# A fused attention and two-MLP kernel: weight preparation, operand splits, input loads and output transposes are given other places in the program

## The chip, the cores and the metric

The kernel runs on one core of a Trainium2 chip. The metric is the device time of one execution in microseconds (us). The program has five instruction streams, one for each engine: PE (TensorE, matmuls and their weight loads), DVE (VectorE), ACT (ScalarE), POOL (GpSimd, here used almost only to issue DMAs) and SP (SyncE, which issues DMAs). Each engine works through its stream in order and waits on semaphores where it needs another's result.

## The reference, cut to what matters

```python
def _attn_ref(q, k, v, mem_k, mem_v):          # 4 x 8 heads, 768 positions, 64 wide, in chunks of 32
    ...                                        # softmax over 16 left, 32 own, 8 right and 8 memory positions

def _moe_ref(x, w_gate, w_val, w_out, rms_g):  # 3072 tokens x 512, d_ff 1536
    xn = x / np.sqrt(np.mean(x * x, axis=-1, keepdims=True) + 1e-06) * rms_g
    g = xn @ w_gate
    return (g * (1.0 / (1.0 + np.exp(-g))) * (xn @ w_val) @ w_out)

def _moe2_ref(x, w_in, w_out):                 # d_ff 2048
    h = x @ w_in
    g = np.where(h >= 1, h, np.where(h <= -1, 0.0, (h + 1) ** 2 / 4.0))
    return g @ w_out
```

The output of the attention goes through the first MLP and then through the second. The weights arrive as 64-bit floats and are turned into 32-bit floats on the chip. For accuracy every 32-bit operand x is split into a high part and a rest, x = hi + lo, and a product takes three matmuls: hi·hi, hi·lo and lo·hi.

## The kernel before, in words

The 3072 tokens are six tiles of 512 (`NTT` = 6). The program runs through these stages:

1. An opening stage with the attention of the first tokens (a hand-written list, `ORDER`).
2. Tiles 0 to 3, one by one, through the first MLP (lines 847 to 876). A tile has 12 column blocks f; a block is 12 matmuls of 128x512 for the gate, 12 for the values and 12 for the output of the block before. Each block has three slots (`slot`, line 767), in which attention steps for later tiles and background steps are laid between the matmuls. Tiles 1 to 3 make 108 slots.
3. Tiles 4 and 5 as a pair through the first MLP. A pair uses a scheme with seven instead of eight products of half-size blocks (Strassen in Winograd's form), for which sums of operands must be formed. The projection has 12 blocks of seven products of six matmuls (`seven`, `proj1`); the output has 7 x 6 blocks of six matmuls (`Out.run`).
4. Three pairs of tiles through the second MLP, each with 8 projection blocks of seven products (`proj2`) and 7 x 8 output blocks.

**Background steps.** The weights of stages 3 and 4 have to be converted, split and summed, and stored in DRAM in the order of the seven products. This work is a list of 376 steps (`steps`, filled by `w1_steps`, `w1o_steps` and `w2_steps`). `conv_step(n)` adds n to a counter and runs as many steps as are due. A slot of tiles 1 to 3 adds `PACE`, a product of stage 3 adds `PACE2`; what remains runs in one go at line 1122. A period of 28 steps prepares one column block and one row block of the second MLP: four loads of 512 KB by POOL (line 276), conversions on ACT and DVE (lines 289, 142 to 148), splits (292, 295), sums (197 to 207), and stores by POOL (303, 209). Loads reuse three buffers `w64`, conversions three buffers `tu`, so a load waits for the stores out of its buffer, and a conversion for the stores out of `tu`. All this stands in the same in-order streams as the work of the products.

**A projection block** (`seven`, line 900). PE makes products 0 and 3; ACT copies the first from PSUM bank A into bank B (line 908), and product 4 is accumulated on top of it, so PE's third product waits for this copy. ACT also copies the second product (line 909), DVE adds (912, 915), and `proj2` then forms the piecewise function with DVE clamps (945), ACT squares (946) and DVE maxima (950). At its end a block issues the load of the weights for the block after the next (`load_wp`, line 799, 1.8 MB, two buffers).

**An output stage** (`Out.run`). Before a block's six matmuls, its operand h is split by ACT (993) and DVE (995) into a ring of buffers, a few blocks ahead; the first ones are split by `ahead` (999) before the last projection block. `load_wo` (815) loads weights four pairs of blocks ahead. Between blocks stand the steps of `x_steps`, which form the sums and splits of the next pair's input y; they are spread by the queue `xq`. The input of the next pair is loaded by `load_y` (793, twice 1 MB on SP) after the projection. Each pair's output is four quarters (j, o), which `turn` (1076) transposes on PE and writes to DRAM: two during the output stage, two after the first two projection blocks of the next pair.

## Time and profile before

| | us |
|---|---|
| median of 3 runs | 1230.75 (1229.84 to 1232.29) |
| the profiled execution | 1235.12 |
| span of its instructions | 1233.3 |
| PE busy | 1149.3 (93%) |
| DVE busy | 865.9 (70%) |
| ACT busy | 619.9 (50%) |
| POOL busy | 155.1 (13%) |

Busy time of PE is not PE at its peak: matmuls overlap, and one that follows a gap or runs at the lower clock counts as longer. More is read from the time that equal numbers of matmuls take in different stages, and from what PE waited for between two of them. Idle time of another engine matters only where PE waits for it in the end.

### The profile page before, as it was taken

How to read it: one execution, taken by the hardware profiler on the slowest of the kernel's cores; microseconds unless marked ns; L12 is line 12 of the kernel's file. 1: busy time of each engine (PE TensorE's matmuls, PEld its weight loads, DVE VectorE, ACT ScalarE, POOL GpSimd, SP SyncE). 2: the span in 40 equal slices, each digit the busy share in tenths (PEclk: the TensorE clock that was granted, in tenths of full speed). 3: DMA queues.
4: the chain of work that ended last, by engine and by line, in shares of the span. 5: the costliest groups of instructions: out<-in, count | busy, mean ns of one | idle time of the engine just before them, and what ended most of it. 6: DMA issues, size and time to landing. Idle time of an engine off the chain costs nothing.

```text
span 1233.3 us, 20567 instructions
## 1 busy us (share of the span) xinstructions
PE 1149.3 (93%) x7909; PEld 919.7 (75%) x7909; DVE 865.9 (70%) x1494; ACT 619.9 (50%) x1096; POOL 155.1 (13%) x239
## 2 busy tenths in 40 slices
PE   6889999999999999787797999989999899999998
PEld 4677877777777788566575768868878778777786
DVE  5889766576657668666568767787757878567855
ACT  4676756565567655333333634446433455334453
POOL 2200012222222332222322000000000000000000
PEclk8899999999999999899998999999999999999999
DMA  8566377788776866998878675566754576653465
GB/s 294 186 204 207 122 266 258 243 283 280 257 269 226 264 222 209 310 357 297 306 262 327 215 247 188 200 247 192 207 185 180 186 249 184 196 186 151 123 196 160
DMA packets 93969, 281.77 MB, mean 228 GB/s; under 512 B 11440, under 2 KB 34480, under 8 KB 87472
## 3 DMA queue, kind: packets, MB, share of 16 engines
q1 hardware_dynamic: 66992, 207.05, 50.4%
q0 software_dynamic: 19200, 65.03, 14.8%
q10 hardware_dynamic: 7680, 8.39, 2.0%
q8 instruction: 62, 1.02, 0.3%
q14 instruction: 35, 0.29, 0.1%
HBM read 201.26 MB, written 79.17 MB: 227 GB/s over the span
## 4 chain that ended last, share of the span: by engine, by line
PE 65%; DVE 11%; DMA 11%; issue 6%; ACT 4%; POOL 2%; ACTq 0%; SPq 0%; DVEq 0%; POOLq 0%
PE ps_y L1045 11%; PE ps_g L1045 8%; PE ps_g L584 6%; PE ps_g L586 5%; PE ps_g L585 5%; DMA w2p_d<-w 3%; PE ps_y L584 3%; PE ps_y L586 2%; PE ps_y L585 2%; PE ps_b L888 2%; PE ps_g L888 2%; PE ps_b L890 2%; PE ps_b L889 2%; DMA w<-in_w_dram 2%; PE ps_g L890 2%
## 5 line engine op out<-in xcount | busy, mean ns | idle before, releaser
L1045 PE MATMUL ps_y<-r,wo 128*128 128x512 f32 x720 | 173.7, 399 | 10.9 <-DMA wo<-w2o_d 5.4
L1045 PEld LDWEIGHTS ps_y<-r,wo 128*128 128x128 f32 x720 | 137.8, 192 | 43.6 <-ACT ps_g L1006 6.1
L995 DVE TENSOR_TENSOR r<-h,r 128x512 fp32r<-128x512 f32 x180 | 121.4, 687 | 54.6 <-ACT r L993 54.3
L584 PE MATMUL ps_g<-xh,wall 128*128 128x512 f32 x384 | 156.1, 407 | 0.1
L586 PE MATMUL ps_g<-xh,wall 128*128 128x512 f32 x384 | 150.7, 392 | 0.1
L585 PE MATMUL ps_g<-xl,wall 128*128 128x512 f32 x384 | 150.5, 392 | 0.0
L993 ACT ACTIVATE r<-h 128x512 fp32r<-128x512 f32 x180 | 108.3, 625 | 68.4 <-PE ps_y L1045 17.4
L946 ACT ACTIVATE t<-t,half 128x512 f32<-128x512 f32 x96 | 66.9, 720 | 132.7 <-DVE t L945 132.7
L1045 PE MATMUL ps_g<-r,wo 128*128 128x512 f32 x540 | 128.1, 392 | 2.7 <-DVE r L995 1.5
L1045 PEld LDWEIGHTS ps_g<-r,wo 128*128 128x128 f32 x540 | 100.5, 188 | 27.1 <-DVE r L995 4.9
L888 PE MATMUL ps_g<-wall 128*128 128x512 f32 x198 | 80.7, 408 | 23.5 <-ACT ps_g L908 13.5
L888 PE MATMUL ps_b<-wall 128*128 128x512 f32 x202 | 80.6, 399 | 12.6 <-ACT ps_b L908 5.0
L586 PEld LDWEIGHTS ps_g<-xh,wall 128*128 128x128 f32 x384 | 72.6, 189 | 16.3 <-DVE wall L117 0.5
L584 PEld LDWEIGHTS ps_g<-xh,wall 128*128 128x128 f32 x384 | 72.7, 189 | 15.8 <-ACT wall L116 0.3
L585 PEld LDWEIGHTS ps_g<-xl,wall 128*128 128x128 f32 x384 | 72.9, 190 | 13.6
L584 PE MATMUL ps_y<-hh,wall 128*128 128x512 f32 x192 | 78.0, 406 | 3.5 <-ACT hh L116 3.5
L890 PE MATMUL ps_b<-wall 128*128 128x512 f32 x202 | 79.6, 394 | 0.0
L889 PE MATMUL ps_b<-wall 128*128 128x512 f32 x202 | 79.4, 393 | 0.0
L889 PE MATMUL ps_g<-wall 128*128 128x512 f32 x198 | 78.4, 396 | 0.0
L890 PE MATMUL ps_g<-wall 128*128 128x512 f32 x198 | 78.4, 396 | 0.0
L585 PE MATMUL ps_y<-hl,wall 128*128 128x512 f32 x192 | 75.7, 394 | 0.2 <-DVE hl L117 0.2
L586 PE MATMUL ps_y<-hh,wall 128*128 128x512 f32 x192 | 75.7, 394 | 0.0
(183 smaller groups left out, 2143.9 us busy)
## 6 DMA issues: line engine op xcount, KB each, us to landing
wo<-w2o_d SPq DMA_DIRECT2D x88, 512.0 KB, 3.6
wall<-w2p_d SPq DMA_DIRECT2D x24, 1792.0 KB, 7.3
wall<-w1p_d SPq DMA_DIRECT2D x12, 1792.0 KB, 9.7
w<-in_w_dram SPq DMA_DIRECT2D x36, 512.0 KB, 3.8
w<-in_w_dram POOLq DMA_DIRECT2D x32, 512.0 KB, 5.5
k_in<-in_k_dram SPq DMA_DIRECT2D x48, 256.0 KB, 4.7
wo<-w1o_d SPq DMA_DIRECT2D x21, 512.0 KB, 4.4
v_in<-in_v_dram SPq DMA_DIRECT2D x40, 260.0 KB, 3.9
```

The source lines that it names most:

```text
L584: nc.tensor.matmul(ps, wh, xh, start=start, stop=False)
L585: nc.tensor.matmul(ps, wh, xl, start=False, stop=False)
L586: nc.tensor.matmul(ps, wl, xh, start=False, stop=stop)
L888: nc.tensor.matmul(bank, wh, xh, start=st, stop=False, skip_group_check=True)
L889: nc.tensor.matmul(bank, wh, xl, start=False, stop=False, skip_group_check=True)
L890: nc.tensor.matmul(bank, wl, xh, start=False, stop=kk == 1, skip_group_check=True)
L946: nc.scalar.activation(s, s, AF.Square, scale=0.5, bias=half)
L993: nc.scalar.activation(r[:, 0], src, AF.Copy)
L995: tt_(out=r[:, 1], in0=src, in1=r[:, 0].bitcast(F32), op=ALU.subtract)
L1045: nc.tensor.matmul(bank[p][m], a, b, start=s0, stop=s1, skip_group_check=True)
```

## The change

- `PACE` goes from 2.4 to 2.8 and `PACE2` from 1.25 to 0.9: more background steps in the slots of tiles 1 to 3, fewer in the products of the pair in stage 3.
- `ahead` now splits one block per call, and is called after single projection blocks: in stage 3 after blocks 3, 5, 7 and 9, in stage 4 after blocks 3 to 6. The ring of stage 3 has five buffers instead of four, and its temporary tiles are six instead of seven.
- `load_y` and the first of the x steps are called during the projection: the load after block 5 in stage 3 and after block 3 in stage 4, the first step after the last block in stage 3 and after block 6 in stage 4.
- `turn` handles half a quarter and returns a function that copies and stores it. Three quarters are now turned in the pair's own output stage. The fourth is transposed after the first two blocks of the next projection, and its copies are put off (`defer`) to a place behind the two ACT copies of the following block.

```diff
@@ -33,8 +33,8 @@
 PT = 256
 D = 64
 FILL = 352
-PACE = 2.4
-PACE2 = 1.25
+PACE = 2.8
+PACE2 = 0.9
 
 
 @with_exitstack
@@ -895,7 +895,7 @@
         m2["n"] += 1
         return m2["t"][m2["n"] % len(m2["t"])]
 
-    banks = []
+    banks, defer = [], []
 
     def seven(n, early):
 
@@ -907,6 +907,8 @@
         p5 = tmp2("p5")
         nc.scalar.activation(B, A, AF.Copy)
         nc.scalar.activation(p5, C, AF.Copy)
+        while defer:
+            defer.pop(0)()
         product(n, B, 4, 1, False)
         product(n, A, 1, 4, False)
         tt(out=C, in0=p5, in1=B, op=ALU.add)
@@ -996,8 +998,8 @@
             if p == 0:
                 tt_(out=B11, in0=B12, in1=B11, op=ALU.add)
 
-        def ahead(self):
-            for n in range(len(m2["ring"]) - 1):
+        def ahead(self, n):
+            if 0 <= n < len(m2["ring"]) - 1:
                 self.split(n)
 
         def run(self, A, B, C, extra):
@@ -1073,21 +1075,28 @@
             else:
                 nc.scalar.activation(d, bank[m], AF.Copy)
 
-    def turn(pr, j, o, ps):
-
-        for q in range(2):
-            for b in range(2):
-                for m in range(2):
-                    c = m2["c"][j][m][:, (2 * q + b) * P:(2 * q + b + 1) * P]
-                    nc.tensor.transpose(ps[q][:, (2 * b + m) * P:(2 * b + m + 1) * P], c, ident)
+    def turn(pr, j, o, q, ps):
+
+        for b in range(2):
+            for m in range(2):
+                c = m2["c"][j][m][:, (2 * q + b) * P:(2 * q + b + 1) * P]
+                nc.tensor.transpose(ps[:, (2 * b + m) * P:(2 * b + m + 1) * P], c, ident)
+
+        def store():
             d = tmp2("os")
             if q:
-                nc.vector.tensor_copy(d, ps[q])
+                nc.vector.tensor_copy(d, ps)
             else:
-                nc.scalar.activation(d, ps[q], AF.Copy)
+                nc.scalar.activation(d, ps, AF.Copy)
             r0 = (2 * pr + o) * TT + 2 * q * P
             dst = out[r0:r0 + 2 * P, 256 * j:256 * j + 256].rearrange("(b p) c -> p b c", p=P)
             nc.scalar.dma_start(dst, d.rearrange("p (b c) -> p b c", b=2))
+
+        return store
+
+    def turns(pr, j, o):
+        for st in [turn(pr, j, o, q, ps_y[q]) for q in range(2)]:
+            st()
 
     out1(*pend)
     while live:
@@ -1097,14 +1106,14 @@
     pair1 = moe1_only.enter_context(ExitStack())
     m2["pool"] = pair1.enter_context(tc.tile_pool(name="p1", bufs=1, reuse_waits="tile"))
 
-    def second_pool(K, n_ring):
+    def second_pool(K, n_ring, n_t):
         new = lambda shape, name, dt=F32: m2["pool"].tile(shape, dt, name=name)
-        m2["t"], m2["n"] = [new([P, TT], f"t{i}") for i in range(7)], 0
+        m2["t"], m2["n"] = [new([P, TT], f"t{i}") for i in range(n_t)], 0
         m2["ring"] = [new([P, 2, TT], f"r{i}", F32R) for i in range(n_ring)]
         m2["h"] = new([P, K, 2, 2, TT], "h")
 
     m2["late"] = m2["pool"].tile([P, 2, TT], F32, name="s1234")
-    second_pool(F1 // 2, 4)
+    second_pool(F1 // 2, 5, 6)
     pair_bank.close()
     bpool = ctx.enter_context(
         tc.tile_pool(name="bpool", bufs=1, space=bass.MemoryType.PSUM, side="right", reuse_waits="tile")
@@ -1116,17 +1125,19 @@
         load_wo(i)
     o1 = Out(F1 // 2, 0, done1, xq)
     for f in range(F1):
-        if f == F1 - 1:
-            o1.ahead()
         proj1(f)
+        if f % 2:
+            o1.ahead(f // 2 - 1)
+        if f == 5:
+            load_y(y_d[0], y_d[1])
+            xq.extend(x_steps())
     conv_step(len(bg))
-    load_y(y_d[0], y_d[1])
-    xq.extend(x_steps())
+    xq.pop(0)()
     o1.run(Y[0:2], [b1, b2], Y[2:4], ())
 
     moe1_only.close()
     m2["pool"] = ctx.enter_context(tc.tile_pool(name="m2", bufs=1, reuse_waits="tile"))
-    second_pool(G2, 5)
+    second_pool(G2, 5, 7)
     m2["c"] = [[m2["pool"].tile([P, TT], F32, name=f"c{j}{m}") for m in range(2)] for j in range(2)]
     n1, n2 = 7 * F1 // 4, 7 * G2 // 2
     for i in range(4):
@@ -1135,18 +1146,22 @@
         banks[:] = b3, Y[3], b4, b1, b2
         o2 = Out(G2, n1 + n2 * pr, done2, xq)
         for g in range(G2):
-            if g == G2 - 1:
-                o2.ahead()
             proj2(G2 * pr + g)
+            o2.ahead(g - 3)
             if pr and g < 2:
-                turn(pr - 1, g, 1 - g, Y[0:2])
-        if pr + 1 < NP2:
-            load_y(y_d[2 * pr + 2], y_d[2 * pr + 3])
-            xq.extend(x_steps())
-        extra = [(5 * G2 + 3, lambda: turn(pr, 0, 0, Y[0:2])), (6 * G2 + 3, lambda: turn(pr, 1, 1, Y[0:2]))]
+                defer.append(turn(pr - 1, 1, 0, g, Y[g]))
+            if g == 3 and pr + 1 < NP2:
+                load_y(y_d[2 * pr + 2], y_d[2 * pr + 3])
+                xq.extend(x_steps())
+            if g == 6 and xq:
+                xq.pop(0)()
+        extra = [
+            (5 * G2 + 2, lambda: turns(pr, 0, 0)),
+            (5 * G2 + 6, lambda: turns(pr, 1, 1)),
+            (6 * G2 + 3, lambda: turns(pr, 0, 1)),
+        ]
         o2.run(Y[0:2], [b1, b2], Y[2:4], extra)
-    turn(NP2 - 1, 0, 1, Y[0:2])
-    turn(NP2 - 1, 1, 0, [b3, b4])
+    turns(NP2 - 1, 1, 0)
     region.close()
 
 
```

The stream of SP around the load of the next pair's input, in the first pair of stage 4, before (`y` is the input, `wall` holds the projection's weights, `wo` the output's):

```order
L799 DMA wall<-w2p_d_125 128x3584
L799 DMA wall<-w2p_d_126 128x3584
L799 DMA wall<-w2p_d_127 128x3584
L799 DMA wall<-w2p_d_120 128x3584
L799 DMA wall<-w2p_d_121 128x3584
L793 DMA y<-y_d_112 128x2048
L793 DMA y<-y_d_113 128x2048
L815 DMA wo<-w2o_d_128 128x1024
L815 DMA wo<-w2o_d_129 128x1024
```

The same place in the changed kernel:

```order
L799 DMA wall<-w2p_d_125 128x3584
L793 DMA y<-y_d_112 128x2048
L793 DMA y<-y_d_113 128x2048
L799 DMA wall<-w2p_d_126 128x3584
L799 DMA wall<-w2p_d_127 128x3584
L799 DMA wall<-w2p_d_120 128x3584
L799 DMA wall<-w2p_d_121 128x3584
L815 DMA wo<-w2o_d_128 128x1024
L815 DMA wo<-w2o_d_129 128x1024
```

The two loads of y stood between the last weights of the projection and the first new ones of the output; now four loads of projection weights stand behind them.

The stream of ACT at the end of the same projection, before (`r` is the ring of split operands, `t` are temporary tiles, 908 is the copy that PE's third product of a block waits for):

```order
L946 ACTIVATE t_7298<-t_7298,half 128x512
L993 ACTIVATE r_7305<-h 128x512
L993 ACTIVATE r_7306<-h 128x512
L993 ACTIVATE r_7307<-h 128x512
L993 ACTIVATE r_7308<-h 128x512
L908 ACTIVATE ps_g_108<-ps_b_5971 128x512
L909 ACTIVATE t_7299<-ps_y_773 128x512
```

The changed kernel from block 3 of that projection on (993 is now line 995, 946 is 948):

```order
L995 ACTIVATE r_7311<-h 128x512
L908 ACTIVATE ps_g_109<-ps_y_773 128x512
L909 ACTIVATE t_7304<-ps_g_108 128x512
L948 ACTIVATE t_7305<-t_7305,half 128x512
L948 ACTIVATE t_7306<-t_7306,half 128x512
L948 ACTIVATE t_7307<-t_7307,half 128x512
L948 ACTIVATE t_7308<-t_7308,half 128x512
L995 ACTIVATE r_7312<-h 128x512
L908 ACTIVATE ps_y_773<-ps_b_6073 128x512
```

Four copies in a row ahead of one block's first copy became one ahead of each of four blocks' first copies.

The stream of ACT from the first to the second projection block of the second pair, before (`os` tiles of the transposed output are also taken from `t`):

```order
L946 ACTIVATE t_7301<-t_7301,half 128x512
L1087 ACTIVATE t_7302<-ps_y_770 128x512
L1090 DMA out_dram<-t_7302 128x2x256
L1090 DMA out_dram<-t_7303 128x2x256
L908 ACTIVATE ps_b_5970<-ps_g_108 128x512
L909 ACTIVATE t_7304<-ps_g_109 128x512
```

The same place in the changed kernel:

```order
L948 ACTIVATE t_7309<-t_7309,half 128x512
L908 ACTIVATE ps_b_6073<-ps_g_108 128x512
L909 ACTIVATE t_7310<-ps_g_109 128x512
L1090 ACTIVATE t_7304<-ps_y_770 128x512
L1093 DMA out_dram<-t_7304 128x2x256
```

The copy and its DMA moved from ahead of the block's two copies to behind them, and the DMA of the other half, which DVE copies, stands one block later.

## Rows read from the trace of the kernel before

**Rows 1.** Windows by stage: length, busy (count) by engine, granted clock, DMA share

```profile
core 0: us, PE busy (x) PEld busy (x) DVE busy (x) ACT busy (x) POOL busy (x), PEclk, DMA share, GB/s
152.70:506.50 353.80, 347.71 (x3486) 278.20 (x3485) 239.86 (x465) 204.63 (x387) 90.45 (x143) 1.00 0.76 255
506.50:660.80 154.30, 126.95 (x505) 98.66 (x504) 91.97 (x163) 54.17 (x98) 42.69 (x67) 0.94 0.82 301
660.80:731.50 70.70, 62.76 (x253) 47.73 (x252) 55.76 (x82) 36.41 (x58) 4.30 (x6) 0.98 0.75 250
731.50:811.70 80.20, 76.88 (x337) 62.94 (x337) 56.86 (x93) 32.02 (x52) 0.00 (x0) 1.00 0.55 199
811.70:895.10 83.40, 80.48 (x354) 65.65 (x353) 64.27 (x94) 44.31 (x72) 0.00 (x0) 0.98 0.71 229
895.10:980.00 84.90, 79.22 (x354) 64.40 (x353) 58.10 (x95) 32.96 (x54) 0.00 (x0) 1.00 0.49 172
...
1148.20:1226.40 78.20, 78.20 (x355) 64.85 (x354) 53.38 (x83) 39.41 (x65) 0.00 (x0) 1.00 0.60 175
```

**Rows 2.** Windows of single projection blocks, same columns

```profile
572.70:583.40 10.70, 9.69 (x44) 7.71 (x42) 7.53 (x15) 4.49 (x8) 1.26 (x2) 1.00 1.00 364
...
769.70:779.20 9.50, 9.50 (x43) 7.87 (x42) 6.76 (x12) 3.85 (x7) 0.00 (x0) 1.00 0.53 193
798.20:811.70 13.50, 10.18 (x43) 7.73 (x43) 11.80 (x20) 5.91 (x11) 0.00 (x0) 1.00 0.38 136
...
905.40:917.30 11.90, 10.75 (x53) 8.63 (x52) 7.38 (x13) 4.35 (x7) 0.00 (x0) 1.00 0.60 200
917.30:928.40 11.10, 9.91 (x45) 7.90 (x44) 6.57 (x12) 3.86 (x7) 0.00 (x0) 1.00 0.64 213
```

**Rows 3.** What PE waited for, 506.5 to 661: us, times, longest

```profile
PE ps_y L888 <- ACT ps_y L908: 5.3, 2, 4.5
```

**Rows 4.** Timeline of POOL, 535 to 560: start, us, [idle before <-releaser]

```profile
545.20 0.57 POOL L276 DMA_DIRECT2D w<-in_w_dram  x1 [7.54 <-DMA w2o_d<-w]
```

**Rows 5.** Timeline of ACT, 548 to 565

```profile
557.80 0.67 ACT L289 ACTIVATE tu<-w 128x512 f32<-128x512 f32 x1 [6.31 <-DMA w2o_d<-tu]
```

**Rows 6.** Landing of line 799's loads, 506 to 650

```profile
DMA to landing us min/median/max: 7.9/9.7/12.7
```

**Rows 7.** Landing of line 799's loads, 730 to 810

```profile
DMA to landing us min/median/max: 6.9/7.1/7.5
```

**Rows 8.** Landing of line 276's loads, 355 to 480

```profile
DMA to landing us min/median/max: 3.7/4.6/8.5
```

**Rows 9.** Landing of line 276's loads, 506 to 650

```profile
DMA to landing us min/median/max: 4.2/7.5/10.6
```

**Rows 10.** Windows of the last blocks of tile 3, columns as Rows 1

```profile
473.40:481.50 8.10, 8.10 (x37) 6.71 (x36) 7.61 (x11) 2.64 (x5) 3.79 (x6) 1.00 0.75 247
...
489.70:506.50 16.80, 13.09 (x50) 10.12 (x49) 14.20 (x24) 6.97 (x12) 4.12 (x7) 0.90 0.93 319
```

**Rows 11.** Timeline of ACT, 967.6 to 972, last projection block of stage 4's second pair

```profile
968.35 2.18 ACT L993 ACTIVATE r<-h 128x512 fp32r<-128x512 f32 x4
```

**Rows 12.** Timeline of PE, 968.9 to 972

```profile
971.06 0.50 PE L888 MATMUL ps_g<-wall 128*128 128x512 f32 x1 [1.68 <-ACT ps_g L908]
```

**Rows 13.** Group of the page: busy, mean ns | idle before, releaser

```profile
L995 DVE TENSOR_TENSOR r<-h,r 128x512 fp32r<-128x512 f32 x180 | 121.4, 687 | 54.6 <-ACT r L993 54.3
```

**Rows 14.** Timeline of SP, 811 to 824

```profile
812.34 0.86 SPq L793 DMA_DIRECT2D y<-y_d  x2
814.64 8.48 SPq L815 DMA_DIRECT2D wo<-w2o_d  x4
```

**Rows 15.** Timeline of PE, 822 to 827

```profile
825.53 1.95 PE L1045 MATMUL ps_y<-r,wo 128*128 128x512 f32 x6 [2.76 <-DMA wo<-w2o_d]
```

**Rows 16.** Window of the second product of that output stage, columns as Rows 1

```profile
825.50:838.10 12.60, 12.57 (x48) 10.26 (x49) 7.24 (x12) 5.54 (x10) 0.00 (x0) 0.86 0.62 198
```

**Rows 17.** Timeline of ACT, 905.8 to 910, second projection block of that pair

```profile
908.92 0.58 ACT L908 ACTIVATE ps_b<-ps_g 128x512 f32<-128x512 f32 x1 [1.90 <-DVE t L1085]
```

## The prediction, made before the changed kernel was run

> **What bounds the kernel now.** I first read the windows by stage, since an equal number of matmuls is the measure that lets stages be compared. The cleanest unit is a projection block of the second MLP: 42 matmuls in 9.5 us at full clock (2.4 GHz, share 1.00), 0.227 us each, with PE never stopping [rows 2]. Against that unit (block 9.52, so 12 blocks 114.3, 8 blocks 76.2; 252 output matmuls 57.1, 336 of them 76.2) the stages lose the following [rows 1]. The pair in the first MLP loses 154.3 − 114.3 = 40.0 in its projection and 70.7 − 57.1 = 13.6 in its output. In the second MLP the first projection loses 4.0 and the second 8.7 (the third repeats the second), the first output stage 7.2 (the second repeats it), and the last output stage only 2.0. Tiles 1 to 3 keep PE busy for 347.7 of 353.8. So PE bounds the tiles and the middle of every later stage; the losses are where stages meet, and all over the pair's projection.
>
> Then I read the waits there. In the pair's projection the causes form a chain. POOL waits 7.54 us until a store has left a weight buffer [rows 4]; the store of a conversion buffer queued behind that comes late, and ACT waits 6.31 us for it with a conversion [rows 5]; behind the conversion on ACT stands the copy of line 908, for which PE waits up to 4.5 us [rows 3]. Where no such wait falls, a block takes 10.7 us with the DMA engines at share 1.00 [rows 2], and the block's weights take 9.7 us to land (median) against 7.1 in a stage without background steps [rows 6, 7]. The stage thus has two limits: late stores, which stop the in-order engines, and DMA.
>
> **The change part by part.** The counts are from the code. Tiles 1 to 3 have 108 slots: 259 steps become 302. The pair's projection has 84 products: of the 376 steps 105 stood there, 3 ahead of it and 9 in a burst behind it; now 72 remain, none of them in the last block, and the burst is gone.
>
> (a) Pair's projection, 154.3. A smooth block held 84 · 1.25 / 12 = 8.75 steps and filled DMA for 10.7 us; its weights alone are 0.53 · 9.5 = 5.0 [rows 2], so a step costs (10.7 − 5.0) / 8.75 = 0.65 us of DMA. With 84 · 0.9 / 12 = 6.3 steps a block has 5.0 + 6.3 · 0.65 = 9.1 us of DMA, just under PE's 9.52. The interval between a store out of the conversion buffer and its next use is seven steps, from 7/1.25 = 5.6 to 7/0.9 = 7.8 products, so 3.0 us more, half of the worst wait of 6.31. I take 10.0 us for nine blocks (the landing 9.7 plus some 0.3), 9.6 for the last two, 14.0 for the first, whose ACT stream begins with a conversion as before, and 3 for waits that stay, among them the weights queued behind y. Together 126.5, so **−27.8**. Bounds: 118 (all but the first two blocks at the unit) and 140 (all ten middle blocks at 11.2).
>
> (b) Pair's output, 70.7. The burst goes, the splits ahead lie inside the projection, and the ring is one block longer, which gives each split 6 · 0.227 = 1.36 us more. The y load that stood at the start moves too. I leave 2.6 of the 13.6, a little over what the last output stage loses: **−11.0**, bounds −13 and −5.
>
> (c) Loads of y in the second MLP. SP issues y at 812.34 and the output's next weights behind it at 814.64 [rows 14]. They let PE go at 825.53 after 2.76 us idle [rows 15], and then the clock is at half (1.2 GHz) for part of the next product, mean 0.86 [rows 16]. The first output stage takes 83.4 and the last, without a y load, 78.2 [rows 1]; 0.7 of the 5.2 I put to the x steps. Twice 4.5 goes: **−9.0**. What comes late instead are the projection's weights behind y. Until 825.53 the queue had spent 13.2 us from 812.34 on y, the weights issued just ahead of it and one output weight. Projection weights are issued a full block before the block that needs them, and y is followed by a load that is needed only two blocks (19.0 us) after y's issue. 13.2 plus the transfer of 5.0 is 18.2, so the cover is 0.8 us: no cost in the centre, 2.5 per pair if it breaks (bound −4.0 in all).
>
> (d) Splits ahead. The last block takes 13.5 instead of 9.5, a loss of 4.0 in each of three pairs [rows 2]. Four ACT copies took 2.18 us [rows 11] and PE then waited 1.68 for line 908 [rows 12], so at most 0.5 was slack, and a single copy (0.55) costs between 0 and 0.55. DVE gains 2 · 0.69 [rows 13] in blocks where it is busy 6.8 of 9.5 [rows 2], with the two products before its next addition as cover. I take 0.42 a block (a gap in the trace is short of the true one, since the ends of matmuls overlap), 1.7 a pair: 3 · (4.0 − 1.7), **−6.9**, bounds −12 and −4.
>
> (e) Turns. In the second pair, blocks 2 and 3 take 11.9 and 11.1 [rows 2]; of the stage's loss of 8.7 they are 4.0, the last block is 4.0, and the rest, 0.7, is the first block's transposes: 4.7 by the turns. ACT stops 1.90 us for DVE's copy, whose DMA it issues, ahead of line 908 [rows 17]; now both copies stand behind it. Left are eight transposes. A turn of eight in the last output stage is part of a loss of 2.0 for two [rows 1], so 1.0 each: 1.1 instead of 4.7, twice −3.6. A third turn in each of three output stages adds 3 · 1.0. After the last matmul one quarter less is left to transpose and copy, −0.6. Sum **−4.8**, bounds −8 and 0.
>
> (f) Tiles 1 to 3. They get 43 steps more, 28 us of DMA on a share of 0.76 over 353.8 [rows 1], so about 0.84. DVE needs some (7.53 − 4.5 · 0.69) / 8.75 = 0.51 us per step [rows 2, 13], 0.6 us more in each block of 9.8. Loads of raw weights land in 4.6 us there against 7.5 in the pair's stage [rows 8, 9], so the buffers have room. The exception is the end of tile 3, where x steps are laid in as well: DVE is busy 7.61 of 8.1, and the last block takes 16.8 for 48 matmuls (10.9) [rows 10]. There I expect 3 more, elsewhere 1.5: **+4.5**, bounds 0 and +20.
>
> Sum: −27.8 − 11.0 − 9.0 − 6.9 − 4.8 + 4.5 = −55.0. The profiled execution took 1235.1 (span 1233.3 and 1.8 around it) and is 0.36% above the median shown, so 1180.1 becomes 1180.1 · 1230.75 / 1235.12 = 1176.
>
> **The rivals.**
>
> A, slower: the chain of buffers can't follow in the tiles. Load, conversion, split, store and next load run at 259 / 353.8 = 0.73 steps per us there now, and at 105 / 154.3 = 0.68 in the pair's projection, where the waits are. If the rate is a limit of 0.68, the 302 steps need 444 us and the tiles grow by 90; all other terms (−59.5) remain: 1235.1 + 30.5, as median 1261. It decides from 353.8 + 59.5 = 413.3 us for the tiles, that is below 0.73 steps per us. For it: the rate of now is exactly there, and POOL's waits are long in the pair. Against it: in tile 3 a block of 8.1 us holds 7.2 steps, 0.89 per us, and takes no longer than its 36 matmuls (8.2) [rows 10]. Chance 0.05.
>
> B: DMA bounds the pair's projection anyway. If fewer steps do not make the weights land sooner, ten blocks stay at 11.5 to 12.7 (the longest landing, [rows 6]), and (a) gives 10 to 15 instead of 27.8: 1189 to 1194. For it speaks the share of 1.00, against it the landing of 7.1 with the steps absent. The Trainium skill ("DMA: Bandwidth & Descriptors", section "Queues, rings and completion order") says that each DMA engine takes turns, packet by packet, between the queues that have work. By that rule a weight load that meets steady background transfers takes up to twice its time alone, some 14 us, and would not get faster while any step is in flight; the measured 12.7 at most and 9.7 in the median say that this holds in part of a block only. Chance 0.14.
>
> C: the waits for y move into the projections. The cover in (c) is 0.8 us; if it breaks, the block after next waits 2.5 us in two pairs and 4 in the first MLP's pair, with the clock's fall behind it: +9, 1185. Chance 0.13.
>
> D: the change does not do what it says, because the stalls at the stage borders have another cause and the splits merely cost in four blocks what they cost in one: (d) and (e) give nothing, 1188. Against it: the last output stage, which has no y behind it, loses 2.0 in all [rows 1]. Chance 0.05.
>
> **How the numbers follow.** The forecast (0.63) has its own range of 1164 to 1187: the terms' bounds do not fall on one side together. B, C and D reach to 1196, A to 1261. Below, all favourable bounds make about 1160. A range of 1160 to 1199 leaves A and the worst of B outside, under 2 in 10. About 0.2% is what a measurement of this kernel can tell from no change. Slower is A, 0.05; about the same needs A at its deciding point, 0.02; faster is the rest, 0.93.
>
> **What would show it.** (a) Projection of the pair near 126 us, ACT's conversions waiting for DMA under 3 us, no wait of POOL over 5. (b) About 60 us. (c) No wait for the output's weights in the first two output stages, which take about 80, and the block two after y without a gap. (d) Blocks 5 to 8 of a projection 9.5 to 10.1 each and no block of 13. (e) Second and third blocks under 10.3; the last output stage a microsecond longer. (f) Tiles 1 to 3 at 356 to 360 us. The prediction is wrong if the tiles grow by more than 15 us or the pair's projection stays over 140.

## The result, and the profile after

The changed kernel takes 1202.33 us (median of 4 runs, 1196.16 to 1203.79), the kernel before on the same chip 1231.52 (4 runs, 1229.84 to 1236.04): ratio 0.9748, 95% interval 0.9705 to 0.9791. It is faster, by 29 us instead of the 55 forecast, and lies 3 us above the top of the range. The profiled execution took 1202.5 us, its span 1200.8.

The stages of the changed kernel, as windows with the columns of [rows 1]; the first line is tiles 1 to 3, then projection and output of the first MLP's pair, the second MLP's three pairs as a whole, and out of these the first projection, first output, second projection and last output.

```profile
152.30:517.90 365.60, 350.98 (x3485) 278.92 (x3484) 261.27 (x507) 214.14 (x404) 108.14 (x169) 0.99 0.79 270
517.90:654.80 136.90, 121.51 (x505) 97.13 (x504) 76.73 (x133) 47.88 (x86) 30.68 (x47) 0.95 0.84 302
654.80:718.60 63.80, 60.45 (x254) 46.69 (x254) 49.25 (x70) 33.21 (x54) 0.00 (x0) 1.00 0.69 217
...
718.60:1194.40 475.80, 473.10 (x2106) 385.81 (x2104) 355.11 (x552) 226.27 (x365) 0.00 (x0) 1.00 0.60 201
...
718.60:797.20 78.60, 77.73 (x337) 62.66 (x336) 58.02 (x94) 32.00 (x52) 0.00 (x0) 1.00 0.62 232
797.20:877.10 79.90, 79.67 (x362) 65.40 (x361) 63.35 (x94) 44.55 (x73) 0.00 (x0) 1.00 0.70 219
877.10:956.60 79.50, 78.64 (x346) 63.45 (x345) 58.66 (x95) 32.72 (x53) 0.00 (x0) 1.00 0.55 204
...
1115.30:1194.40 79.10, 79.09 (x362) 65.39 (x361) 54.02 (x84) 39.78 (x66) 0.00 (x0) 1.00 0.59 180
```

The same window over the second MLP before:

```profile
731.50:1226.40 494.90, 474.52 (x2099) 387.80 (x2099) 354.88 (x551) 225.87 (x364) 0.00 (x0) 0.99 0.58 192
```

PE's busy time there has hardly changed (474.5 and 473.1); what went are 18 us of idle time. The terms, measured as differences of windows (profiled executions, 1235.1 and 1202.5):

| term | forecast | measured |
|---|---|---|
| (a) pair's projection | −27.8 | 154.3 to 136.9: −17.4 |
| (b) pair's output | −11.0 | 70.7 to 63.8: −6.9 |
| (c), (d), (e) second MLP, with its tail | −20.7 | 494.9 to 475.8, tail 6.9 to 6.4: −19.6 |
| (f) tiles 1 to 3 | +4.5 | 353.8 to 365.6: +11.8 |
| sum | −55.0 | −32.1 |

The second MLP came as forecast. Of the 23 us that are missing 22 lie in (a), (b) and (f), all three in the first MLP, in stages that hold background steps or x steps.

**Tiles.** What PE waited for in tile 3 of the changed kernel (us in total, times, longest):

```profile
PE ps_y L584 <- ACT hh L116: 2.8, 1, 2.8
PE ps_g L584 <- ACT s L858: 2.1, 2, 1.9
PE ps_a L557 <- DVE e L447: 1.9, 1, 1.9
PE ps_a L557 <- ACT x_nat L544: 1.7, 1, 1.7
```

Before, only the first of these was there (3.5 us). The windows of tile 3, before and after:

```profile
390.20:506.50 116.30, 112.59 (x862) 90.95 (x858) 86.82 (x158) 65.68 (x123) 34.89 (x54) 0.99 0.73 244
```

```profile
393.70:517.90 124.20, 115.30 (x859) 91.47 (x857) 94.31 (x172) 68.51 (x128) 41.81 (x63) 0.97 0.73 253
```

Counted by its gate matmuls, the third of its twelve blocks takes 14.1 instead of 10.0 us, the last three 37.0 instead of 33.1; the others are as before. The third block holds the waits of line 557, the end the other two. Lines 544 and 447 belong to the attention that is laid between the tile's matmuls. ACT at the last wait of the list, timeline rows of 410 to 425:

```profile
416.30 0.42 ACT L292 ACTIVATE w<-tu 128x256 fp32r<-128x256 f32 x1 [2.59 <-DVE tu L148]
416.62 1.32 ACT L544 ACTIVATE x_nat<-x_nat,rs 128x512 f32<-128x512 f32 x2
```

and PE:

```profile
417.38 0.66 PE L557 MATMUL ps_a<-ident,x_nat 128*128 128x128 f32 x4 [1.74 <-ACT x_nat L544]
```

Line 292 is a weight step's copy. It stands ahead of line 544 on ACT and waits 2.59 us for a step's addition on DVE; line 544, which waits for nothing of its own, comes late by that, and PE with it. So what costs here isn't the sum of DVE's busy time (it went from 239.9 to 261.3 in a stretch of 365.6), but a step's hand-over between two in-order engines ahead of a step of the attention.

**Pair's projection.** Windows of some blocks, columns as before:

```profile
529.90:544.90 15.00, 10.01 (x43) 7.62 (x41) 11.11 (x20) 5.64 (x10) 3.58 (x6) 0.91 0.96 362
544.90:556.50 11.60, 11.53 (x42) 9.37 (x43) 2.29 (x4) 3.41 (x6) 3.43 (x5) 0.82 0.75 269
...
577.50:587.00 9.50, 9.50 (x43) 7.88 (x42) 6.16 (x12) 4.08 (x8) 1.28 (x2) 1.00 0.71 248
...
596.70:607.90 11.20, 9.72 (x43) 7.70 (x41) 5.50 (x9) 4.67 (x9) 3.42 (x5) 1.00 1.05 420
...
628.10:645.30 17.20, 12.23 (x43) 9.57 (x42) 9.19 (x16) 5.53 (x10) 3.71 (x6) 0.80 0.55 200
```

Of the twelve blocks (counted from 0) five take 9.5 to 9.7, and three more 11.2 to 11.6 each; two take 15.0 and 17.2. The first of these begins on SP, which stands in the output weights' loads (four from 519.76, the last 13.23 us later) until a store of step buffers has left the space; what SP waited for from 517 to 535, and after it the timeline row of the projection weights queued behind:

```profile
SPq L815 <- DMA w2p_d<-s: 11.2, 2, 10.1
```

```profile
519.76 13.23 SPq L815 DMA_DIRECT2D wo<-w1o_d  x4
533.11 0.38 SPq L799 DMA_DIRECT2D wall<-w1p_d  x1
```

They land 11.8 us later, and PE, in its timeline, waits; the next block then has no wait at all and yet takes 11.6, at a granted clock of 0.82, that is partly at 1.2 GHz:

```profile
544.97 0.80 PE L888 MATMUL ps_b<-wall 128*128 128x512 f32 x1 [4.88 <-DMA wall<-w1p_d]
...
635.94 0.80 PE L888 MATMUL ps_g<-wall 128*128 128x512 f32 x1 [4.97 <-ACT ps_g L908]
```

The second row is the block of 17.2. Its chain begins as that of [rows 3 to 5]: POOL waits for a store, ACT with a conversion for another. POOL, then ACT:

```profile
618.95 0.56 POOL L276 DMA_DIRECT2D w<-in_w_dram  x1 [10.77 <-DMA w2p_d<-w]
```

```profile
628.97 0.66 ACT L289 ACTIVATE tu<-w 128x512 f32<-128x512 f32 x1 [4.16 <-DMA w2p_d<-tu]
...
634.77 0.63 ACT L292 ACTIVATE w<-tu 128x512 fp32r<-128x512 f32 x1 [4.13 <-issue]
635.30 0.58 ACT L908 ACTIVATE ps_g<-ps_g 128x512 f32<-128x512 f32 x1
```

But line 908 doesn't stand right behind the conversion. Between them stands the hand-over seen in the tiles: line 292, a step's copy, waits 4.13 us. The profile names no releaser, but the step's addition on DVE (line 148) ends at 634.68, 0.09 us before; it stands there behind the block's own additions and a split. The same copy waits 2.7 to 5.5 us ahead of line 908 of this block in the versions below with a late y, late output weights, stores that hold no buffer and a shorter step.

In sum PE waits 15.3 us in this stage: 7.4 for line 908, 6.4 for weights, 1.5 for other things. The landing of line 799's loads, 517 to 655, which was 9.7 in the median [rows 6], did not fall:

```profile
DMA to landing us min/median/max: 8.3/10.9/11.8
```

### The profile page after: what moved, and what is told of

It reads as the page before. It is cut to its first block, busy times and chain, and to the rows that moved or that the text cites. A ratio compares the mean times of both kernels' runs of the same rounds, so it can differ in the third digit from the quotient of the medians.

```text
span 1200.8 us, 20562 instructions
## 1 busy us (share of the span) xinstructions
PE 1144.0 (95%) x7909; PEld 915.6 (76%) x7909; DVE 865.3 (72%) x1494; ACT 620.2 (52%) x1096; POOL 156.5 (13%) x239
## 5 line engine op out<-in xcount | busy, mean ns | idle before, releaser
L1047 PE MATMUL ps_y<-r,wo 128*128 128x512 f32 x720 | 169.3, 391 | 2.6 <-DVE r L997 1.6
L1047 PEld LDWEIGHTS ps_y<-r,wo 128*128 128x128 f32 x720 | 134.3, 188 | 33.3 <-DVE r L997 3.3
## 6 DMA issues: line engine op xcount, KB each, us to landing
wall<-w1p_d SPq DMA_DIRECT2D x12, 1792.0 KB, 10.2
```

Of the source, the lines that this page charges most:

```text
L1047: nc.tensor.matmul(bank[p][m], a, b, start=s0, stop=s1, skip_group_check=True)
```

## The experiments

The experiments ran in four groups, each on one chip with the kernel before beside it (median 1232.6, 1230.7, 1231.5 and 1231.3). Windows are of one execution each. Two versions below (y late in the second MLP, x steps earlier) leave the pair's projection as it is in the changed kernel, and yet it takes 138.8 and 140.6 us in their profiles instead of 136.9, its first block 16.3 and 14.5 instead of 12.0, block 10 14.1 and 17.9 instead of 17.2. So a difference of less than some 4 us in that stage shows nothing by itself.

**Which part does what.** Pace alone: the kernel before with `PACE = 2.8`, `PACE2 = 0.9`.

> The kernel before with the two paces of the change alone (2.8 and 0.9); y loads, splits ahead and turns stay as before. Theory S (the background steps cost the tiles what the changed trace shows, 365.6 us against 353.8, and the pair's projection keeps most of its gain): tiles 1 to 3 near 365, the pair's projection near 135, output stage of the pair 65 to 71 (no burst, ring of four), stage 4 unchanged; about 1220 us. Rival Y (the tiles are slowed by nothing but the pace, but the pair's projection of the changed kernel lost some 10 us to the y load in its middle): the pair's projection here, without that y load, is under 130 in spite of the splits' burst at its end; about 1213 us. Rival O (the tiles' growth comes from the other edits): tiles at 354 and about 1208 us.

1221.16 us, ratio 0.9912 (0.9897 to 0.9928). Tiles 1 to 3 take 365.3, the pair's projection 134.2, its output 69.4; the second MLP takes 491.7, 3 less than before. The tiles' growth is all the pace's. The counterpart, the changed kernel with 2.4 and 1.25:

> The changed kernel with the old paces (2.4 and 1.25). Theory S: tiles 1 to 3 back at 354 (-11.8), the pair's projection back to 148 to 152 (+11 to 15, the burst of splits stays away), a burst of nine steps ahead of the pair's output again (+3): 1203 to 1209 us, the pace is worth little in all. Rival N (the pace is a net loss): under 1198 us. Rival P (the pace carries the gain of the pair's stage as predicted): over 1215 us.

1219.86, 0.9895 (0.9872 to 0.9919). Tiles 354.5, projection 158.0, longer than before and than expected: with y in the middle, its blocks 6 to 8 take 14.6, 18.2 and 15.9. Each half alone gives 11 to 13 us, 24 together, and both give 29. What the halves lack lies in the pair's output, not in the projection: the output takes 70.7 before, 69.4 with the pace alone (its second product waits 2.5 us for weights behind y), 72.3 with the other edits alone (its first product takes 16.8, behind the burst of nine steps) and 63.8 with both. In the projection the other edits cost 3.7 at the old pace (154.3 to 158.0) and 2.7 at the new one (134.2 to 136.9), each within the spread of one execution.

**The pair's projection.** y behind it, as before (`load_y` and `x_steps` below the loop, the rest unchanged):

> The changed kernel with the first MLP pair's y load and its first x step behind the projection, as they were. Theory Y (the 2 MB of y, ahead of projection weights on one queue and among the steps' stores, make blocks 7 to 10 late): these blocks, 48.6 us in the changed kernel, fall to 40 or less, the waits of ACT's conversions for stores at 605 and 629 go, the output stage grows by 0 to 3; 1193 to 1197 us. Rival W (the waits come from the steps' own chain of buffers whatever y does): blocks 7 to 10 stay over 46 and the time within 2 us of the changed kernel.

1202.53, 0.9758 (0.9740 to 0.9775): no difference. Blocks 7 to 10 take 43.0 instead of 48.6, but the output 66.5 instead of 63.7 (PE waits 2.5 for its weights behind y) and the first block 14.8 instead of 12.0. With y, blocks 7 to 10 take 48.2 and 49.7 in the two further profiles of the same projection, so this gain of 5 to 6 us holds.

Output weights later:
```
 for f in range(F1):
     proj1(f)
+    if f == 2:
+        for i in range(4):
+            load_wo(i)        # no longer ahead of the loop
```

> The changed kernel with the first four loads of the pair's output weights issued behind the third projection block instead of ahead of the first. Theory F (SP stands in the second of these loads until a store of the pair sums has left the memory under it, 11.2 us in the changed trace, and issues the third block's weights 3 us late): block 2 loses its wait of 4.9 us and the half clock behind it, 6 to 7 us less, 1195 to 1197 us. Rival D (those weights were late because DMA was full, landing 11.8 us after issue): the wait shrinks by 3 at most, 1199 to 1202 us.

1199.53, 0.9744 (0.9723 to 0.9765). SP no longer waits for a step's store; blocks 1 and 2 take 9.8 and 10.2 instead of 15.0 and 11.6. Block 0 takes 16.4 instead of 12.0, and the projection gains 1.7 in all, less than its spread: the wait went as theory F has it, the total is what rival D has.

Stores that hold no buffer: the pair sums' stores outside the first MLP's single stage read a constant tile (`src` replaced by `g_b`, so the stored sums are not the weights').

> The changed kernel in which, from the pair's projection on, the stores of the pair sums read a constant tile instead of the conversion and sum buffers (the stored sums are then wrong): the same DMAs of the same size, but no buffer of a sum or conversion waits for them. Theory C (the pair's projection loses its time to late stores through the in-order ACT and DVE): ACT's conversions no longer wait at blocks 1, 7 and 10 (3.3, 4.7 and 4.2 us), block 10 falls from 17.2 to under 12, the projection from 136.9 to 124 to 130; about 1193 us. Rival Q (the transfers fill the DMA engines, and any load or store is late): the projection stays over 133.

1200.10, 0.9752 (0.9729 to 0.9775), projection 136.2 and not theory C's 124 to 130. ACT's conversions no longer wait for those stores; PE waits 6.5 us for weights, in three blocks (6.4 in two in the changed kernel), and 5.3 for line 908. What PE waited for there:

```profile
PE ps_g L888 <- ACT ps_g L908: 5.3, 2, 3.2
PE ps_y L888 <- DMA wall<-w1p_d: 2.8, 1, 2.8
PE ps_b L888 <- DMA wall<-w1p_d: 2.3, 1, 2.3
...
PE ps_g L888 <- DMA wall<-w1p_d: 1.4, 1, 1.4
```

So the stores of the sums, as holders of buffers, don't make the loss: in block 10 line 292 waits 5.5 us without them. The buffers of raw weights are held here too (POOL waits 38.7 us for their stores, 44.5 in the changed kernel), and no run frees those. No steps in the projection (`conv_step(80 if (t, s) == (1, 0) else PACE)`: they go into the first slot of tile 1):

> Changed kernel with 77 further weight steps in the first slot of tile 1, so that none is left for the pair's projection; its total is no measure, only the projection is (its weights, the output weights and y stay). Theory Q (the steps' transfers and the in-order conversions make all of the projection's loss but the start's): 118 to 121 us, the first block 14 or less with the DMA engines' share near 0.6 in the middle blocks. Rival (the stage's own loads, output weights and y among them, and the bank changes lose most): 127 or more, with the waits for weights in blocks 1 to 2 and 7 as before.

The projection takes 118.5, eleven blocks of 9.5 each, y and the output weights included. Its window, and those of an ordinary block and of the block with y:

```profile
585.80:704.40 118.60, 116.24 (x506) 95.72 (x506) 40.11 (x60) 31.15 (x54) 1.74 (x3) 0.99 0.61 222
599.70:609.20 9.50, 9.50 (x44) 7.86 (x43) 2.67 (x4) 2.38 (x4) 0.00 (x0) 1.00 0.54 193
647.30:656.80 9.50, 9.50 (x44) 7.86 (x43) 4.66 (x7) 2.38 (x4) 0.00 (x0) 1.00 0.89 346
```

The stage's own loads cost it nothing, y among them; all the rest is the steps', alone or by what they meet.

**The tiles.** Pace by tile, `conv_step({1: 3.6, 2: 2.6, 3: 2.5 if s < 21 else 1.8}[t])`:

> The changed kernel with the same number of steps in tiles 1 to 3, spread otherwise: 3.6 per slot in tile 1, 2.6 in tile 2, 2.5 in tile 3 up to block 6 and 1.8 in its last five blocks. Theory V (the tiles grow where DVE's in-order stream is full: in tile 3 with the x steps in it, and where attention steps queue behind background steps; tile 1 has room): tile 1 119 to 122 (118.1), tile 2 119 to 121 (123.3), tile 3 116 to 118 (124.2), together 355 to 360; 1192 to 1197 us. Rival R (a rate limit of the buffers' chain): tile 1 grows by the share of the steps it was given, to 127 and more, and the sum stays at 364 or over.

1209.41, 0.9820 (0.9787 to 0.9853): slower than the changed kernel. Tile 1 takes 130.4 instead of 118.1, with waits of the kind shown above (at the longest, a step's sum on DVE itself waits 2.14 us for a store, which is what rival R named; its numbers came, too, 378.6 for the three tiles); what PE waited for in it:

```profile
PE ps_a L557 <- ACT x_nat L544: 4.8, 2, 3.7
PE ps_a L461 <- DVE x_nat L504: 2.0, 1, 2.0
```

Tile 2 takes 129.1 instead of 123.3, though it was given fewer steps per slot (forecast 119 to 121): PE waits 7.6 us there for copies of the attention. So the steps per slot don't set a tile's time by themselves; with tile 1's higher pace other steps of the list fall into tile 2, but no run here tests whether that is the reason. Tile 3, with fewer steps at its end, takes 119.1. A shorter step: the two later of the three DVE operations that join a weight's words are left out in the second MLP's steps.

> The changed kernel without two of the three DVE instructions that join a raw weight's halves in the second MLP's steps (1.4 us of DVE per raw weight; the weights are then wrong); every DMA, buffer and ACT instruction stays. Theory V: from the middle of tile 2 on DVE has 1.7 us less per block; tile 2 falls to 119 to 121, tile 3 to 116 to 119; the pair's projection falls by a few us only, to 130 to 135. Rival R (waits for stores and loads, which this leaves): tile 2 and 3 stay within 2 us of 123.3 and 124.2.

1194.40, 0.9709 (0.9682 to 0.9736). Tile 3 takes 118.8: its waits for the attention's steps are gone but for 0.2 and its third block takes 10.5, with the count of steps, their loads and stores as in the changed kernel. What stays at its end is a conversion that waits 4.44 us for a store, ahead of line 116:

```profile
PE ps_y L585 <- ACT hh L116: 5.4, 1, 5.4
PE ps_a L558 <- DVE e L448: 0.2, 1, 0.2
```

Tile 2 takes 122.3 (forecast 119 to 121), with 4.0 us of waits as in the changed kernel (4.7), although DVE's busy time in it falls from 83.4 to 73.8. What lengthens tile 2 stays open.

**y in the second MLP.** `load_y` and the x steps behind the projections, as before:

> The changed kernel with the second MLP's y loads and first x steps behind the projections, as before the change. If the prediction's term (c) is right, the first two output stages grow by 4.5 each (79.9 to 84.4), the first with a wait of about 2.8 for the output's weights at the start of the second product and half clock behind it, and the projections give back up to 1 each: 1209 to 1212 us. If the wait had only moved into the projections, the time stays within 3 us of the changed kernel.

1207.99, 0.9819 (0.9799 to 0.9839), 5.7 more. The first two output stages grow from 79.9 to 82.5 and 84.1 (forecast 84.4), and the wait of before is back, the only one that PE has in the second MLP:

```profile
PE ps_y L1047 <- DMA wo<-w2o_d: 5.1, 2, 2.6
```

The projections of these two pairs give back 0.7 each. The second product, behind the wait, in the first and the second pair:

```profile
809.80:820.80 11.00, 11.00 (x49) 9.08 (x49) 7.45 (x12) 5.75 (x10) 0.00 (x0) 1.00 0.70 233
```

```profile
971.10:983.70 12.60, 12.56 (x48) 10.25 (x49) 7.47 (x12) 5.77 (x10) 0.00 (x0) 0.86 0.59 203
```

After the same wait the granted clock fell in one and not in the other, a difference of 1.6 us.

**The price of a step.** Three versions between the paces, all with the output weights late. Fewer steps at the end of tile 3, `conv_step(PACE if t < 3 or s < 21 else 1.8)`, `PACE2 = 1.08`:

> Changed kernel with the four loads of output weights behind the third projection block, and the pace in the last 15 slots of tile 3 at 1.8 instead of 2.8 (15 steps fewer there), 1.08 instead of 0.9 in the pair's projection, which takes them over. Theory S (in tile 3 the steps' copies and additions stand ahead of the attention's steps on the in-order engines): tile 3 falls from 127.2 (with the output weights late) to about 119 to 121. What the 15 steps cost in the pair's projection: theory L (a smooth price per step, worked out from 136.9 at 0.9 and 158.0 at 1.25, 0.72 us a step) 135 + 11 = 146, total 1202; theory T (a threshold: the DMA engines have room up to some 1.1) 135 to 138, total 1192 to 1195.

1200.27, 0.9727 (0.9698 to 0.9756). Its profile is of the fastest of its five runs (1194.8), so its windows flatter it by some 5 us somewhere:

```profile
390.90:505.90 115.00, 111.23 (x866) 89.65 (x858) 85.14 (x155) 64.98 (x120) 35.92 (x55) 1.00 0.70 241
505.90:647.40 141.50, 122.11 (x506) 97.16 (x505) 85.43 (x150) 52.15 (x93) 35.89 (x55) 0.96 0.85 318
```

Tile 3 falls below 116.3 of before; the projection lies between the two theories. The last three blocks of the tile take 27.9 instead of 37.0. Its third block still takes 14.0, with the attention's waits of the changed kernel, so these are not what the lower pace took away:

```profile
PE ps_a L557 <- DVE e L447: 1.8, 1, 1.8
PE ps_a L557 <- ACT x_nat L544: 1.7, 1, 1.7
```

Half way, `PACE = 2.6`, `PACE2 = 1.1`:

> Changed kernel with the four loads of output weights behind the third projection block and the paces half way, 2.6 in the tiles and 1.1 in the pair's projection. If both costs are smooth in the pace: tiles 1 to 3 at 361 (half way from 354.5 to 367.6), projection at 146, total about 1204. If the projection has a threshold above 1.1: projection 136, total 1194. If the tiles have a threshold between 2.6 and 2.8: tiles 356, total 1199 or, with both, 1189.

1209.12, 0.9812 (0.9783 to 0.9842): tiles 362.1, projection 147.7, the smooth case by its stages, though the total is 5 above it. By the room that each tile showed, `conv_step({1: 3.1, 2: 2.8, 3: 2.8 if s < 21 else 1.9}[t])`, `PACE2 = 0.98`:

> Changed kernel with the four loads of output weights behind the third projection block and the pace by the room that the tiles showed: 3.1 in tile 1 (which took 118.1 us at 2.8 as at 2.4, and 130.4 at 3.6), 2.8 in tile 2 and up to slot 20 of tile 3, 1.9 in its last 15 slots; 0.98 in the pair's projection. Some 3 steps fewer in the tiles than in the changed kernel. If a tile has a threshold (theory T): tile 1 at 118 to 119, tile 2 at 122 to 123, tile 3 at 115 to 116, projection 137 to 139, total 1192. If every step above 2.8 costs tile 1 in proportion to what 3.6 cost (12.3 us for 29 steps, 0.42 a step; theory L): tile 1 at 123, total 1197.

1199.65, 0.9743 (0.9721 to 0.9766): tiles 120.6, 124.2 and 117.6, projection 137.3. Tile 1 lies between the two theories, the total above both, and by its interval it is no faster than the changed kernel.

**x steps an output product earlier** (`n >= G` for `n >= 2 * G`):

> Changed kernel; the x steps of an output stage begin with its second product instead of its third. Theory X (the fifth to seventh products of the pair's output, 9.8, 11.8 and 9.6 instead of 8.2 us, wait for splits because the x steps' additions, 1.2 us each, stand on DVE beside the outputs' additions): these products fall to some 8.5, 10.0 and 9.0, the pair's output from 63.7 to about 60 to 61, and the two later output stages with x steps by about 1 each; total 1197. Rival Y (the outputs' additions alone do it): the pair's output stays at 63 to 64, total 1202; if the second product is crowded instead, 1203 to 1204.

1209.08, 0.9814 (0.9785 to 0.9842), slower. In the pair's output the loss moves with the x steps: products three to seven take 8.8, 9.9, 10.7, 8.2, 8.2 instead of 8.2, 8.2, 9.8, 11.8, 9.6, so the x steps make it and the outputs' own additions do not; the stage gains 1.6. But the two later output stages with x steps, where I expected a gain, take 83.8 and 83.6 instead of 79.9: their third products take 15.7 and 14.1 instead of 10.9. In the first, an x step's copy on ACT (line 824) waits 4.14 us for its sum on DVE, and the output's splits stand behind it.

The runs together, as steps that stand in the pair's projection (376 in all, less those that the paces lay ahead of it or behind it) and its time:

| steps | 0 | 72 | 74 | 86 | 93 | 105 |
|---|---|---|---|---|---|---|
| projection, us | 118.5 | 136.9 | 137.3 | 141.5 | 147.7 | 158.0 |

The points at 74, 86 and 93 have the output weights late, and all versions with 72 steps together lie between 132.9 and 140.6. The first 72 cost (136.9 − 118.5) / 72 = 0.26 us each (0.20 to 0.31 with that spread), the 33 from there to the pace of before (158.0 − 136.9) / 33 = 0.64 (0.53 to 0.76). The tiles by steps per slot: tile 1 takes 118.0, 118.1, 120.6 and 130.4 us at 2.4, 2.8, 3.1 and 3.6; tile 3 116.3, 121.7 and 124.2 at 2.4, 2.6 and 2.8. Tile 2 follows no such line: 119.5 at 2.4, 122.3 and 129.1 in two versions at 2.6, 123.3 at 2.8.

## Why the prediction was right in direction and wrong in size

**Right: (c), (d), (e).** In the second MLP the output's weights are no longer waited for; after the change PE waits there for 1.3 us in all. The late y load brings back 5.1 of it, two waits as in [rows 15]; with the clock and the neighbouring stages it costs 5.7 of the 9.0 that I gave (c). Of the 3.3 between them, 1.6 are the clock, which fell behind both waits before and behind one of them here, and 1.4 what moving y costs the two projections (their last blocks take 10.6 instead of 9.9), which I had put at nothing. The blocks with a split take 9.9 to 10.1 (forecast 9.5 to 10.1), the last blocks 9.9 to 10.6 instead of 13.5 [rows 2], the blocks with the turn 9.8 and 10.0 instead of 11.9 and 11.1, and the last output stage is 0.9 longer (forecast 1.0). No run takes the splits or the turns away alone; (d) and (e) rest on these blocks, which stay as they were with the pace alone. The cover of 0.8 us that I worked out for the weights behind y was enough here: rival C did not come in these pairs.

**Wrong in size: (a), −17.4 for −27.8.** The step that failed is the price of the steps that stay. I put a block at 9.1 us of DMA, under PE's 9.52, and so let 6.3 steps a block go for nothing, with "3 for waits that stay" (the blocks as I listed them add up to 126.2, not 126.5). PE's waits came to 15.3 us, and the matmuls kept it busy for 121.5 instead of 114.3 at a mean granted clock of 0.95. Without any step the stage takes 118.5, so the 72 steps cost 18.4. Their price does not begin where DMA is full on average (the share is 0.84 after, 0.82 before): a late store or a late hand-over stops an in-order engine or a queue. In the profiled execution the 10.4 us missing are mostly two blocks. Block 1 (15.0) is the edge that I did not look at: four output weight loads ahead of the loop, which wait on SP for the steps' last stores and hold the projection's weights behind them. It was in the trace of before, where SP waits 11.5 us in them for such a store:

```profile
507.80 13.67 SPq L815 DMA_DIRECT2D wo<-w1o_d  x4
```

Block 10 (17.2) is the hand-over of line 292 to line 148 ahead of line 908. My chain from [rows 3 to 5] went from the late store to line 908 and left it out. How long block 10 gets varies: 14.1 to 17.9 in three profiles of the same projection, 12.6 with y late, 14.4 with the pace alone. That y meets the steps costs some 5 us over blocks 7 to 10 together (48.2 to 49.7 with y, 43.0 with y late and 44.4 with the pace alone, 38.0 with y and no steps). For the first MLP's pair rivals B and C were thus partly right. C's wait for the weights behind y came, with 1.5 us instead of 4. The weights' landing stayed (10.9 against 9.7), as B said, and without steps it is 7.2:

```profile
DMA to landing us min/median/max: 6.9/7.2/8.3
```

But a block's length is not its weights' landing, since they are issued a block ahead; five of twelve blocks ran at the unit all the same, so B's reason for its time does not hold. (Ten blocks of 11.5 to 12.7 would have given (a) 4 to 16 and not 10 to 15.) The Trainium skill ("DMA: Bandwidth & Descriptors", section "Queues, rings and completion order") says that a DMA engine takes turns between the queues that have work; from this B worked out up to twice the time alone. The landing here is 10.9 / 7.2 = 1.5 times, which stays under that estimate and shows no more.

**Wrong in size: (b), −6.9 for −11.0.** Burst and splits went as forecast: the first four products take 8.2 each. I left 2.6 for the rest, as if the x steps went away with the y load. This is the step that failed: they stay beside the fifth to seventh products, which lose 6.6 (7.7 before), and the loss moves where the x steps are moved.

**Wrong in size: (f), +11.8 for +4.5.** Two thirds of the growth are in tile 3 (+7.9; tile 2 +3.8, tile 1 +0.1). Its end grew by 3.9, near the 3 that I had there; the step that failed is the 1.5 for all the rest. The third block of tile 3 alone grew by 4.1, before 427, where no x step stands. I priced DVE's busy time and the buffers' room; what decides in that block is that a step's copy waits for another engine ahead of the attention's own copy, and a step shorter by two DVE operations takes these waits away. A lower pace in the last 15 slots takes away the growth of the end instead. What lengthens tile 2 is not shown. My bound of 20 held (f). Rival A is refuted: 302 steps in 365.6 us are 0.83 per us, over the 0.73 of before, and the tiles did not grow by 90. Rival D is refuted by the second MLP.

**Why the time lies above the range.** (a), (b) and (f) each stayed inside their bounds, but all three on the bad side. The range leaned on "the terms' bounds do not fall on one side together". These three have one kind of cause, follow-up work that stands in in-order streams ahead of what PE needs (steps in (a) and (f), x steps in (b)), so they fell on one side together, by 21.8 us.

What stays open is the first block of the projection: it takes 12.0, 14.5 and 16.3 us in kernels that are the same up to there, 19.0 with the shorter step and 13.8 without steps. Whether what is saved in tile 3 or in block 1 comes back there is not shown with such a spread. No version that keeps all the work was found that is faster than the changed kernel beyond the runs' spread: 1199.5, 1199.7 and 1200.3 have intervals that overlap its own.

## What to carry to other kernels

Background work in an in-order stream is priced by what it stops, not by the mean share of the engine or of DMA: look for the copy that waits for another engine and for the queue entry that waits for a store, and see which foreground step stands behind it. What a piece of it costs differs from stage to stage and rises with the rate (tile 1 took 2.8 steps per slot free and 3.6 for 12 us; tile 2 cost more at 2.6 in one version than at 2.8 in another), so measure the stage that work is moved into, and take the load that meets the background work (here y) into the same sum. Terms that miss for one reason miss together, so a range must not let them cancel. When a stall is removed, count the remaining work of that place again at its new position; here the load went and its follow-up steps stayed.

## What the runs showed of the hardware

A DMA share of 1.00 in a window is no ceiling: before, a block showed 1.00 at 364 GB/s [rows 2]; the block with y shows 1.05 at 420. I had taken 1.00 for full. And a wait of PE can cost more than its length, but need not: after 4.88 us idle the following block, without a wait, took 2.1 us over its unit at a granted clock of 0.82; after two waits of some 2.6 us for the output's weights the following product took 12.6 us at 0.86 in one pair and 11.0 at 1.00 in the other.
